# Filler products of TensorE in a planned attention and gated-MLP kernel: one for every 180 planned idle nanoseconds in place of one for every 300

## The chip, the cores and the metric

The kernel runs on one core of one Trainium2 chip. The metric is the device time of one execution in microseconds (us); less is better. The engines of a core are named here as the profile names them: PE is the matmul unit (PEld its weight loads), DVE the vector engine, ACT the scalar engine, POOL is GpSimd, and SP only issues transfers (DMAs) between the main memory and the core's SBUF. Each engine takes its instructions strictly in the order of the program and waits for others through semaphores.

## What is computed

The reference is an attention with a local window and block summaries, and behind it a two-layer MLP in which half of the hidden units are mixed along the sequence and multiplied into the other half. The shapes are batch 4, 8 heads, sequence 768, head size 64; model width 512, hidden width 1024.

```python
# attention, per batch and head
k_sum = k.reshape(B, H, nb, 32, D).max(axis=3)
v_sum = v.reshape(B, H, nb, 32, D).mean(axis=3)
scores_l = where(|i - j| < 16, scale * q @ k.T, -1e9)
scores_s = scale * q @ k_sum.T + log(32)
a = softmax(concat([scores_l, scores_s]))
x = a @ concat([v, v_sum])                 # heads side by side: (4, 768, 512)
# MLP
h = relu(x @ w_in); u, v = h[..., :512], h[..., 512:]
v_n = (v - mean(v)) / sqrt(var(v) + 1e-6)
v_s = w_spatial @ v_n + b_spatial[:, None]
out = (u * v_s) @ w_out
```

## The kernel before

The kernel does not issue its instructions as it goes. It records every operation (a block of matmuls, one vector instruction, one DMA) in a plan, with an estimated duration for each engine that can do it, and then writes the operations out in an order that a long string of characters (`ORDER`) fixes, engine and all. For each operation the plan also keeps a start and an end by its own estimates; they do not change the order, since the order is listed.

For each batch, the attention goes in groups: a group is 256 rows of the sequence and four heads. A group has a block of scores on PE (named s, line 497: 16 small products of q and k), a softmax on DVE (line 510, reading the scores), ACT (line 514, the exponential) and POOL, DVE or ACT (line 527 or 525, the division), a transposition on PE (t, lines 546 and 554), and the product with the values on PE (x, line 570). Then come the MLP's products in float32 split into a high and a low part, three matmuls for one (line 604): pv and pu are the two halves of `x @ w_in`, sp the product with `w_spatial`, po the one with `w_out`.

At the start of the program, before the first MLP product can run, PE has only a few small things to do, and they need transfers and preparations:

- s_0_0, the scores of the first group, needs two blocks of keys (k), into which ACT copies block maxima (line 414), and a block of queries (qd).
- s_1_0 are the scores of a second group. Its queries go to the same buffer as those of s_0_0, so SP issues their load only when s_0_0 is done.
- wwi_3, wwi_1, wwi_0 and wwi_2 are short products (lines 314 to 316) that help to split pieces of `w_in`.
- s_0_1 needs another block of queries (in the second buffer, qd_127 below) and two more blocks of keys.
- vsum (line 441) are sums of the values over blocks, in two halves of 12 products each, read from tiles vn; ACT spreads the result into the tile ve (line 457), which x_0_0 needs. From x_0_0 come xh and xl (lines 273 and 585), which the first pv needs.

SP's loads wait in one row: a load behind one that waits does not start either.

Where the plan sees PE idle between two operations, it puts filler products into PE's row: an identity matrix times its own first 120 columns, into a PSUM tile named warm that nobody reads. The first such product is an operation of its own (line 798) and so is the last (line 869, recorded in the loop over groups, which bounds the stretch of the program in which fillers are put); those between them are written in this loop, at line 910:

```python
    for op in plan.order():
        if op.eng == "PE":
            if warm.made is not None and op.start < warm.ops[-1].start:
                for _ in range(int((op.start - idle - (WARM_0 if idle < WARM_0 else 0)) * WARM)):
                    nc.tensor.matmul(out=warm.t[:, :KW], lhsT=ident, rhs=ident[:, :KW], start=True, stop=True)
            idle = op.end
        op.fn(op.eng)
```

Here `op.start` and `idle` are the plan's estimates in ns, `WARM` is the number of fillers for one ns of planned idle time, and `WARM_0` is taken off the first wait. The profile counts two records for each filler product, since a float32 matmul is done in two passes there.

Of the kernel before, what the change touches and what calls it, by code (L numbers as in the profile page):

```python
# [925 lines left out]
PACE_0, PACE, DENSE_0, STRETCH = 12.13, 15.16, 59.674, 1.249  # L926
WIN_V, WIN_U, WSP_AT, WO_AT = -10.0, 46.367, 71.69, 99.123
VT_OFF, VM_OFF, KP_OFF = 7.652, 3.17, -8.814
WARM, WARM_0, WARM_TO = 1 / 300, 3400.0, 1
ON_PE = (0, 1, 2, 3)  # L930
PAIRED_FROM, HALVED_FROM, AFTER = 6, 2, 8.0
KEEP_AT, MIX_AT = 90.0, 2.0
# [150 lines left out]
```

## Time and profile before

| | |
|---|---|
| time, median of 3 runs | 392.02 us (391.38 to 392.37) |
| the profiled execution's own time | 392.32 us |
| its span, first to last instruction | 390.6 us |
| mean granted TensorE clock over the span | 0.996 |
| busy share: PE, DVE, ACT, POOL | 97%, 74%, 56%, 36% |
| records of filler products (lines 798, 910, 869) | 2, 78, 2 |

The span is what the profile's clock sees between the first and the last instruction; the time of an execution has 1.7 us more around it. Times in the trace count from the span's start. A busy time of PE counts overlapping records once, and the duration of one matmul record includes its passage through the array, so two that follow each other start closer together than either lasts. Where a stretch of the first 6.7 us is asked for, the granted clock reads 1.00 because the record of the clock begins later; the pace of the products tells it there.

### The profile page before, as it was taken

Reading aid. Unit: us, or ns where it says so; the run is one execution under the profiler, and the core shown is the slowest. Engines: PE = TensorE matmul, PEld = TensorE weight load, DVE = VectorE, ACT = ScalarE, POOL = GpSimd, SP = SyncE. Lnnn points to the kernel's source line nnn. Section 1 sums busy time; section 2 is a strip of 40 time slices with the busy share of each in tenths; the row PEclk is TensorE's granted clock in tenths of the full one; section 3 lists DMA queues with packets and bytes.
Section 4 is the critical chain, followed back from the end, with each engine's and each line's share of the span. In section 5 each row is a group of like instructions: output and inputs, shape, how many; then the busy total and the mean of one; then the engine's idle time right before and its main releaser. Section 6 shows DMA issues by size and latency. Waiting matters only on the chain.

```text
span 390.6 us, 9728 instructions
## 1 busy us (share of the span) xinstructions
PE 380.1 (97%) x3547; PEld 331.0 (85%) x3547; DVE 289.6 (74%) x990; ACT 218.2 (56%) x699; POOL 139.6 (36%) x157
## 2 busy tenths in 40 slices
PE   8978999999999999999999999999999999999996
PEld 7656778899989888899897888899998878899985
DVE  3987999999847799975777677886597656754830
ACT  3977998996764594567444493272357454210011
POOL 4222566612532447254051033357345142221210
PEclk9989999999999999999999999999999999999999
DMA  8997868857477898889954795558871343049413
GB/s 312 297 271 213 255 216 273 241 173 221 132 233 259 284 284 295 292 254 309 309 190 165 222 256 180 143 145 253 292 200 27 121 153 109 0 159 306 141 68 122
DMA packets 41983, 81.77 MB, mean 209 GB/s; under 512 B 4560, under 2 KB 17360, under 8 KB 41936
## 3 DMA queue, kind: packets, MB, share of 16 engines
q1 hardware_dynamic: 41792, 81.02, 65.8%
q8 instruction: 28, 0.46, 0.5%
q14 instruction: 19, 0.16, 0.1%
q10 hardware_dynamic: 144, 0.13, 0.1%
HBM read 66.58 MB, written 14.55 MB: 208 GB/s over the span
## 4 chain that ended last, share of the span: by engine, by line
PE 91%; DMA 4%; DVE 2%; ACT 1%; issue 1%; SPq 1%; POOL 0%; ACTq 0%; DVEq 0%; POOLq 0%
PE sp L604 22%; PE pv L604 17%; PE pu L604 17%; PE po L604 16%; PE x L570 6%; PE s L497 5%; PE t L554 3%; DMA qd<-in_qT_dram 2%; PE warm L910 2%; DMA tr<-mixed_w 2%; PE vsum L441 1%; SPq L267 1%; ACT ve L457 0%; DVE vs L652 0%; DVE p L510 0%
## 5 line engine op out<-in xcount | busy, mean ns | idle before, releaser
L514 ACT ACTIVATE p<-p,sums 128x120 f32<-128x120 f32 x192 | 73.9, 387 | 29.4 <-DVE sums L510 29.0
L510 DVE CUSTOM_DVE_ANT_0 p<-s,mask 128x120 f32<-128x120 f32 x192 | 45.9, 275 | 17.7 <-PE s L497 17.5
L604 PE MATMUL pu<-xh,win_h 128*128 128x256 f32 (+1 forms) x128 | 43.5, 340 | 0.4 <-DVE c L746 0.4
L604 PE MATMUL pu<-xl,win_h 128*128 128x256 f32 (+1 forms) x128 | 43.0, 336 | 0.0
L604 PE MATMUL pu<-xh,win_l 128*128 128x256 f32 (+1 forms) x128 | 43.0, 336 | 0.0
L604 PE MATMUL po<-wo_h,gh 128*128 128x512 f32 (+1 forms) x100 | 38.7, 387 | 0.2 <-DVE ob L273 0.2
L604 PE MATMUL pv<-win_h,xh 128*128 128x512 f32 x96 | 38.7, 403 | 0.0
L604 PE MATMUL po<-wo_l,gh 128*128 128x512 f32 (+1 forms) x100 | 38.2, 382 | 0.0
L604 PE MATMUL po<-wo_h,gl 128*128 128x512 f32 (+1 forms) x100 | 38.2, 382 | 0.0
L604 PE MATMUL pv<-win_h,xl 128*128 128x512 f32 x96 | 37.6, 392 | 0.3 <-DVE xl L585 0.3
L604 PE MATMUL sp<-tr,vnh 128*128 128x384 f32 x144 | 37.3, 339 | 0.4 <-DMA tr<-mixed_w 0.4
L604 PE MATMUL pv<-win_l,xh 128*128 128x512 f32 x96 | 37.5, 391 | 0.0
L514 ACT ACTIVATION_READ_ACCUMULATOR p<-p,sums 128x1 f32 x192 | 36.4, 189 | 0.0
L604 PE MATMUL sp<-tr,vs 128*128 128x384 f32 x162 | 30.8, 337 | 0.0
L527 POOL TENSOR_TENSOR p<-p,sums 128x480 f32<-128x480 f32 x20 | 19.7, 991 | 29.2 <-DVE wi L299 9.3
L639 POOL TENSOR_TENSOR mv<-mv,mhalf 128x1 f32<-128x1 f32 x24 | 13.5, 566 | 44.4 <-DVE mv L638 43.6
L277 ACT ACTIVATE u<-pu 128x384 f32<-128x384 f32 (+2 forms) x36 | 13.3, 385 | 28.4 <-PE pu L604 27.2
L570 PEld LDWEIGHTS x<-pt,ve 120*64 120x64 f32 x768 | 23.8, 138 | 5.9 <-issue 5.3
L604 PEld LDWEIGHTS sp<-tr,vs 128*128 128x128 f32 x162 | 27.7, 188 | 0.6 <-DMA tr<-plain 0.4
L604 PEld LDWEIGHTS pu<-xh,win_h 128*128 128x128 f32 x128 | 24.1, 189 | 3.8 <-DVE c L746 0.7
L570 PE MATMUL x<-pt,ve 120*64 120x64 f32 x768 | 25.8, 224 | 1.1 <-issue 1.1
L604 PEld LDWEIGHTS sp<-tr,vnh 128*128 128x128 f32 x144 | 25.5, 188 | 1.4 <-DMA tr<-mixed_w 0.7
(174 smaller groups left out, 935.1 us busy)
## 6 DMA issues: line engine op xcount, KB each, us to landing
tr<-mixed_w SPq DMA_DIRECT2D x36, 384.0 KB, 4.3
tr<-plain SPq DMA_DIRECT2D x27, 384.0 KB, 4.3
k<-in_kext_dram SPq DMA_DIRECT2D x16, 544.0 KB, 5.2
qd<-in_qT_dram SPq DMA_DIRECT2D x24, 256.0 KB, 3.5
ve<-in_vext_dram SPq DMA_DIRECT2D x23, 256.0 KB, 5.2
out_dram<-ob SPq DMA_DIRECT2D x23, 256.0 KB, 2.3
vt<-in_vT_dram SPq DMA_DIRECT2D x48, 96.0 KB, 3.0
wi<-in_w_in_dram SPq DMA_DIRECT2D x7, 512.0 KB, 6.3
```

The costliest lines, as they stand in the source:

```text
L267: add(("SP", issue), lambda e: nc.sync.dma_start(out=out_() if callable(out_) else out_, in_=in_() if callable(in_) else in_), pri, w, r, ...
L277: nc.scalar.activation(out=out_, in_=in_, func=AF.Relu)
L441: nc.tensor.matmul(out=ps.t[pr * SBLK:pr * SBLK + NS, :P], lhsT=vs_one[:, o:o + NS], rhs=vn[t].t[:, pr * P:(pr + 1) * P], start=t == 0, st ...
L497: nc.tensor.matmul(out=ps.t[r * QB:(r + 1) * QB, a, i * KW:(i + 1) * KW], lhsT=qt[hs, r, i], rhs=kts[r].t[hs, g * SEG:g * SEG + KW], start ...
L510: add(("DVE", 203), lambda e, i=i, mi=mi: nc.vector.tensor_tensor_reduce(out=pt.t[:, i, :], in0=ps.t[:, a, i * KW:(i + 1) * KW], in1=mask[ ...
L514: add(("ACT", 380), lambda e, i=i: nc.scalar.activation(out=pt.t[:, i, :], in_=pt.t[:, i, :], func=AF.Exp, scale=-1.0, bias=st.t[:, 0, i:i ...
L527: eng(e).tensor_tensor(out=pt.t, in0=pt.t, in1=st.t[:, 0, :BPU].unsqueeze(2).broadcast_to([P, BPU, KW]), op=ALU.mult)
L554: nc.tensor.transpose(out=ps.t[:KW, r, a * CH + i * QB:a * CH + (i + 1) * QB], in_=pts[a].t[hs, i, :], identity=ident[hs, hs])
L570: nc.tensor.matmul(out=ps.t[a * D:(a + 1) * D, r, n * QB:(n + 1) * QB], lhsT=win(buf, n, o), rhs=rhs(n, a, r), start=True, stop=True)
L604: nc.tensor.matmul(out=ps.t[:, :n], lhsT=x, rhs=y, start=(j == i == 0), stop=(j == last and i == 2))
L639: add(("POOL", 560), lambda e: nc.gpsimd.tensor_tensor(out=mv.t[:, 1:2], in0=mv.t[:, 1:2], in1=mhalf, op=ALU.pow), pri, w=[mv])
L910: nc.tensor.matmul(out=warm.t[:, :KW], lhsT=ident, rhs=ident[:, :KW], start=True, stop=True)
```

## The change

One number in a table of constants is changed: the plan puts a filler product into PE's row for every 180 ns of planned idle time, and not for every 300 ns.

```diff
 PACE_0, PACE, DENSE_0, STRETCH = 12.13, 15.16, 59.674, 1.249
 WIN_V, WIN_U, WSP_AT, WO_AT = -10.0, 46.367, 71.69, 99.123
 VT_OFF, VM_OFF, KP_OFF = 7.652, 3.17, -8.814
-WARM, WARM_0, WARM_TO = 1 / 300, 3400.0, 1
+WARM, WARM_0, WARM_TO = 1 / 180, 3400.0, 1
 ON_PE = (0, 1, 2, 3)
```

Apart from the fillers, each engine has the same instructions in the same order; only the numbers in buffer names differ. Line 910 gives 39 products before and 66 with the change, in these places of PE's row: 19 and 31 before s_0_0, 5 and 9 behind it, 7 and 12 behind s_1_0, 4 and 6 behind the first half of t_0_0, 4 and 7 behind the first half of vsum, and 0 and 1 before the first product of pv_0.

The start of PE's row, before the change (s_0_0 is the block of scores of the first group, wwi_3 a helper product for the weights):

```order
L798 MATMUL warm<-ident 128x120
L910 MATMUL warm<-ident 128x120 x19
L497 MATMUL s_0_0_181<-k_0_136,qd_126 64x120
...
L910 MATMUL warm<-ident 128x120 x5
L314 MATMUL wwi_3_0_222<-wi_2_138,ident 128x512
```

And with the change:

```order
L798 MATMUL warm<-ident 128x120
L910 MATMUL warm<-ident 128x120 x31
L497 MATMUL s_0_0_193<-k_0_136,qd_126 64x120
...
L910 MATMUL warm<-ident 128x120 x9
L314 MATMUL wwi_3_0_238<-wi_2_138,ident 128x512
```

Nothing changed its place; 12 products more stand between the start and s_0_0, and 4 more behind it.

Further down PE's row, from t_0_0 (the transposition of the first group's softmax) to wwi_2, before the change (s_0_1 is the third block of scores, vsum the sums of values from tiles vn):

```order
L546 MATMUL t_0_0_330<-ident,p_0_0_1_205 120x128 x4
L910 MATMUL warm<-ident 128x120 x4
L497 MATMUL s_0_1_349<-k_2_144,qd_127 64x120
...
L546 MATMUL t_0_0_330<-ident,p_0_0_0_200 120x128 x4
L441 MATMUL vsum<-vn_236,vs_one 24x128 x2
L441 MATMUL vsum<-vn_212,vs_one 24x128 x2
L441 MATMUL vsum<-vn_273,vs_one 24x128 x2
...
L910 MATMUL warm<-ident 128x120 x4
L314 MATMUL wwi_2_0_421<-wi_2_138,ident 128x512
```

And with the change:

```order
L546 MATMUL t_0_0_351<-ident,p_0_0_1_217 120x128 x4
L910 MATMUL warm<-ident 128x120 x6
L497 MATMUL s_0_1_372<-k_2_144,qd_127 64x120
...
L546 MATMUL t_0_0_351<-ident,p_0_0_0_212 120x128 x4
L441 MATMUL vsum<-vn_252,vs_one 24x128 x2
L441 MATMUL vsum<-vn_224,vs_one 24x128 x2
L441 MATMUL vsum<-vn_289,vs_one 24x128 x2
...
L910 MATMUL warm<-ident 128x120 x7
L314 MATMUL wwi_2_0_447<-wi_2_138,ident 128x512
```

Two products more stand before s_0_1, three more before wwi_2; vn_273 of before is vn_289 now.

SP's row of loads near the start, which the change leaves as it is but for buffer numbers (in brackets what a load waits for: PE is the end of s_0_0, whose queries the load of qd_126 overwrites; the DMAHW entries are earlier loads):

```order
L267 DMA k_2_144<-in_kext_dram 128x1088
L267 DMA qd_126<-in_qT_dram 128x512 [waits DMAHW3_49,PE_49]
L267 DMA vt_0_0_207<-in_vT_dram 128x192 [waits DMAHW0_49]
L267 DMA vn_212<-in_vnat_dram 128x512 [waits DMAHW1_49]
L267 DMA wi_2_138<-in_w_in_dram 128x1024 [waits DMAHW2_49]
L267 DMA k_3_228<-in_kext_dram 128x1088
L267 DMA vn_232<-in_vnat_dram 128x256 [waits DMAHW4_49]
L267 DMA vn_236<-in_vnat_dram 128x512 [waits DMAHW5_49]
L267 DMA qd_127<-in_qT_dram 128x512 [waits DMAHW6_49]
```

Nothing moved in this row. The load of qd_127, which s_0_1 reads, is the seventh behind the load that waits for s_0_0.

## Rows read from the trace of the kernel before

**Rows 1.** The page, part 1: busy time, share of the span, instructions.

```profile
PE 380.1 (97%) x3547; PEld 331.0 (85%) x3547; DVE 289.6 (74%) x990; ACT 218.2 (56%) x699; POOL 139.6 (36%) x157
```

**Rows 2.** Waits of PE from 40 us on: total, times, longest, us.

```profile
PE pu L604 <- DVE c L746: 0.4, 1, 0.4
PE sp L604 <- DMA tr<-mixed_w: 0.4, 1, 0.4
PE x L570 <- issue: 0.4, 1, 0.4
PE po L604 <- DVE ob L273: 0.2, 1, 0.2
```

**Rows 3.** Timeline of PE, 0 to 36.8 us: start, length, instruction, [idle before].

```profile
2.29 6.54 PE L910 MATMUL warm<-ident 128*128 128x120 f32 x38
8.76 1.05 PE L497 MATMUL s<-k,qd 64*64 64x120 f32 x32
9.74 1.38 PE L910 MATMUL warm<-ident 128*128 128x120 f32 x10
10.95 1.03 PE L314 MATMUL wwi<-wi,ident 128*128 128x512 f32 x2
...
12.88 1.05 PE L497 MATMUL s<-k,qd 64*64 64x120 f32 x32 [0.43 <-DMA qd<-in_qT_dram]
13.86 1.82 PE L910 MATMUL warm<-ident 128*128 128x120 f32 x14
15.52 1.03 PE L314 MATMUL wwi<-wi,ident 128*128 128x512 f32 x2
...
18.49 0.65 PE L546 MATMUL t<-ident,p 128*120 128x128 f32 x4 [0.16 <-POOL p L527]
18.98 1.05 PE L910 MATMUL warm<-ident 128*128 128x120 f32 x8
22.48 1.17 PE L497 MATMUL s<-k,qd 64*64 64x120 f32 x32 [2.45 <-DMA qd<-in_qT_dram]
...
24.43 2.76 PE L441 MATMUL vsum<-vn,vs_one 128*24 128x128 f32 x24
27.12 1.19 PE L910 MATMUL warm<-ident 128*128 128x120 f32 x8
28.15 1.03 PE L314 MATMUL wwi<-wi,ident 128*128 128x512 f32 x2
...
29.56 1.50 PE L441 MATMUL vsum<-vn,vs_one 128*24 128x128 f32 x24
31.79 1.25 PE L570 MATMUL x<-pt,ve 120*64 120x64 f32 x32 [0.73 <-issue]
...
36.05 0.50 PE L604 MATMUL pv<-win_h,xl 128*128 128x512 f32 x1 [0.35 <-DVE xl L585]
```

**Rows 4.** Timeline of ACT: the later of two copies of maxima into k.

```profile
8.15 0.42 ACT L414 COPY k<-gm 128x288 f32<-128x288 f32 x1
```

**Rows 5.** Windows, line 910 alone: stretch, its length, busy (records), granted clock.

```profile
2.60:6.40 3.80, 3.80 (x20) 3.80 (x20) 1.00 0.96 372
7.00:8.40 1.40, 1.40 (x15) 1.40 (x14) 1.00 1.03 416
```

**Rows 6.** Windows, PE alone: stretch, its length, busy (records), granted clock, DMA share.

```profile
23.85:27.20 3.35, 3.35 (x29) 0.50 1.00 256
27.25:31.00 3.75, 3.75 (x36) 1.00 0.85 242
```

**Rows 7.** Timeline of SP: the load of qd behind s_0_0's end.

```profile
9.87 0.33 SPq L267 DMA_DIRECT2D qd<-in_qT_dram  x1
```

**Rows 8.** The chain that ended last, 0 to 60 us: start, length, what.

```profile
13.09 9.25 DMA qd<-in_qT_dram
```

**Rows 9.** Tile vn, loads issued from 21 to 21.5 us, and their time to landing.

```profile
L267 SPq DMA_DIRECT2D vn<-in_vnat_dram x1: 328/328/328, 21.1 to 21.1; - x1
...
DMA to landing us min/median/max: 3.7/3.7/3.7
```

## Prediction

> **What bounds the kernel now.** I read four things in this order: how busy PE is, what it waits for once the MLP runs, its timeline over the first 37 us, and the clock it was granted there. PE is busy for 380.1 us of the span of 390.6 [rows 1]. From 40 us on it waits four times for anything that the profile names, 1.4 us in all (0.4 + 0.4 + 0.4 + 0.2) [rows 2]. So behind 40 us there is almost nothing into which a delay could sink: if the first pv starts d later, the end is about d later too. The fillers all lie before that, and their price is what they do to the start of x_0_0 and, through it, of pv.
>
> Over the first 37 us the reader should look for the idle time in brackets: 0.43 us before s_1_0, 0.16 before t_0_0, 2.45 before s_0_1, 0.73 before x_0_0 and 0.35 inside the first pv [rows 3]. There is none before s_0_0: the fillers run from 2.29 us up to it, and it starts at 8.76. The last of its operands in the rows is ACT's copy into k, which ends at 8.15 + 0.42 = 8.57 us [rows 4]. So the 19 fillers of before fill the wait for s_0_0 to within 0.2 us.
>
> **What one filler costs.** Of the rows at the full clock, the group of 14 records takes 15.52 - 13.86 = 1.66 us until the next instruction and the group of 10 takes 10.95 - 9.74 = 1.21 [rows 3]: 0.45 us for 4 records, 0.1125 each, 0.225 us a product. At the start the pace is slower: 3.8 us hold 20 records there, against 15 in 1.4 us later [rows 5], which is the ratio of the two clock levels, 1.2 and 2.4 GHz. The added 12 come last in their group, behind the time at which the pace has doubled, so I cost them at 0.225. At the slow pace (some 0.42 a product, from the same 3.8 us) they would cost 5.0 us and not 2.7; that is the upper bound of this term.
>
> **The change, place by place**, each shift against the rows of before:
>
> 1. 12 fillers before s_0_0: 12 x 0.225 = 2.70 us, with no idle time to hide them. s_0_0 starts at 11.46.
> 2. The load of the second qd_126 waits for s_0_0's end and holds up all of SP's row behind it. Its issue moves from 9.87 [rows 7] to 12.57.
> 3. 4 fillers more behind s_0_0, 0.90: wwi_3 is 3.60 late, s_1_0 can go at 12.45 + 3.60 = 16.05. Its queries took 12.88 - 9.87 = 3.0 us from issue to use [rows 3, 7] and are there by 15.6. The wait of 0.43 is gone; s_1_0 is 3.17 late.
> 4. 5 fillers more, 1.13: wwi_1 and wwi_0 are 4.30 late. t_0_0's operand comes from a softmax that follows s_0_0, about 18.49 + 2.70 = 21.2, ahead of PE at 18.33 + 4.30 = 22.63; the 0.16 is gone too, and t_0_0 is 4.14 late.
> 5. 2 fillers more, 0.45: PE is ready for s_0_1 at 22.48 - 2.45 + 4.14 + 0.45 = 24.62, where it was ready at 20.03.
> 6. s_0_1 waits for qd_127, issued at 13.09 and landed 9.25 us later, at 22.34 [rows 8]. This issue stands behind that of point 2, so it moves by up to 2.70. The loads between start on emptier queues now, which gives something back; no row shows how much. At one end nothing is given back, 2.70. At the other the load goes as freely as that of point 3 (3.0 us): then it lands before PE wants it, and PE's 24.62 sets s_0_1. I take 2.5, near the first end, since 9.25 us between issue and landing say that the loads ahead of it fill the time, and they all move alike. It lands at 24.84 and s_0_1 starts at about 24.98, 2.50 late, with an idle time of 0.4 in place of 2.45.
> 7. What is given back: the idle time before s_0_1 is followed by a stretch at a granted clock of 0.50, 23.85 to 27.20, and 1.00 after it [rows 6]; these are 1.2 and 2.4 GHz. From s_0_1's start to the end of the first half of vsum is 27.12 - 22.48 = 4.64 us there. At the full clock the same takes 0.98 (s, as 9.74 - 8.76) + 0.49 (t, 18.98 - 18.49) + 1.50 (the second half of vsum) = 2.97 [rows 3]. Keeping the clock is worth 1.67 us, and with the idle time at 0.4 I expect it kept.
> 8. But vsum's third tile is the vn load issued at 21.1 and landed 3.7 later, at 24.8 [rows 9]. Moved by 2.5, it lands at 27.3; PE wants it at 24.98 + 0.98 + 0.49 + 0.50 = 26.95 and waits 0.35. The first half of vsum ends at 28.30, 1.18 late.
> 9. 3 fillers more, 0.68: wwi_2 and the second half of vsum are 1.86 late, and with them ACT's spreading, x_0_0 and pv.
> 10. The one before pv_0, 0.225 us, lies inside the wait of 0.35 for xl [rows 3]. Without that cover it would cost its 0.225.
>
> The sum is 2.70 + 0.90 - 0.43 + 1.13 - 0.16 + 0.45 = 4.59 on PE up to s_0_1, less 2.09 of the idle time there (2.45 - 0.36), less 1.67 of clock, plus 0.35 of a new wait, plus 0.68: **1.86 us**. The profiled execution took 392.32 us, 0.30 over the median of the runs; by its own time the changed kernel gives 394.2, and against the median 393.9. With the loads at their free end, PE sets s_0_1 at 24.62, the wait in point 8 goes, and the sum is (24.62 - 22.48) - 1.67 + 0.68 = 1.15. With the loads 2.70 late it is 2.06.
>
> **A rule against this forecast.** PE's long idle time comes before a stretch at half the clock [rows 3, 6]. The Trainium skill (TensorE: Matmul & The Clock Gate, "Why this matters for your kernels") advises to keep TensorE busy between bursts, because it falls to the low clock when it idles. By that advice alone, denser fillers win the 1.67 us; the trace agrees about the clock and disagrees about the fillers being free, since s_0_0 has no idle time before it. The result it would give is the last rival.
>
> **The rivals.**
>
> - *The clock falls all the same.* The waits of 0.4 and 0.35 us might come together with more, if vn lands later than I take it. Then point 7 is lost: 1.86 + 1.67 = 3.5 us, 395.5. For it: the rows don't tell how short an idle time is short enough. Against: the idle time shrinks from 2.45 to under 1. Chance 0.14. The upper bound of the first term lies in its direction too: with the clock rising later than in this execution, up to 2.3 us more (5.0 - 2.7).
> - *No measurable change.* The loads behind s_0_0 catch up and the clock is kept, 1.15 us; and if the clock rises a microsecond or two earlier than in this execution, the longer first group gains about half of that, where before s_0_0 could not start ahead of its operands: 392.0 to 393.1. For it: emptier queues. Against: the 9.25 us of qd_127's load. Chance 0.23.
> - *Faster.* The fillers lie in waits, as the plan meant, and the clock is kept. It needs s_0_0's operands to come 2.7 us later than in this trace, so that the first 12 cost nothing: 1.15 - 2.70 = -1.55, 390.5. From operands 2.4 us later on the sum is past -1.2, faster. Against it: the copy at 8.15 follows loads that nothing in the change touches. Chance 0.05.
>
> **How the numbers follow.** The forecast as worked out (1.15 to 2.06, that is 393.2 to 394.1) has 0.58. A measurement of this kernel can tell about 0.3%, 1.2 us, from no change. The forecast lies above that mark, with its lower end on it: I count 0.52 of its 0.58 as slower and 0.06 as the same. Slower is then 0.52 + 0.14 = 0.66, the same 0.06 + 0.23 = 0.29, faster 0.05. The range leaves out the faster case and the upper end of the first rival: 392.4 to 395.8.
>
> **What would show it.** In the profile of the changed kernel: s_0_0 at about 11.5 us, directly behind the fillers; the second qd load issued near 12.6; s_0_1 near 25.0 with under 1 us of idle time before it; a granted clock of 1.00 from 22 to 30 us; vsum's first half under 2.2 us long; x_0_0 near 33.6 in place of 31.79; and from there the same waits as before. The prediction is wrong if s_0_0 starts before 10.5 us (its operands, not the fillers, held it), if qd_127 lands within 1.5 us of 22.34 (the loads caught up), if the 0.50 stretch is there again, or if x_0_0 is late by what I say and the end is not, which would mean that PE's waits behind 40 us hide more than the rows name.

## The result, and the profile after

The changed kernel takes 394.50 us (median of 9 runs, 393.73 to 395.67) against 390.25 for the kernel before (9 runs, 388.99 to 392.37, the three known beforehand among them): a ratio of 1.0097, 95% interval 1.0077 to 1.0118. Run again later beside other kernels (e9 below) it took 393.44 against 391.04, a ratio of 1.0065 (1.0041 to 1.0089). So it is slower, by 0.4 to 1.2% with both intervals taken together. The forecast was 393.9, a loss of 1.86 us. The measured time lies in its range, but the loss by medians is 4.25 us the first time and 2.40 the second. That 394.50 comes near 393.9 is luck: the three runs known beforehand lay in the upper part of what the kernel before does, so the forecast started 1.77 us too high (392.02 in place of 390.25), and its loss was 2.39 too small.

The profiled execution of the changed kernel took 394.12 us, 1.80 more than that of before. The page has PE busier by 4.9 us [rows 1] and a granted clock of 0.9 or more in every slice; over the span its mean is 1.00:

```profile
PE 385.0 (98%) x3601; PEld 336.1 (86%) x3601; DVE 289.2 (74%) x990; ACT 217.7 (55%) x699; POOL 139.7 (36%) x157
...
PEclk9999999999999999999999999999999999999999
```

The timeline of PE, beside [rows 3]:

```profile
2.28 9.09 PE L910 MATMUL warm<-ident 128*128 128x120 f32 x62
11.30 1.05 PE L497 MATMUL s<-k,qd 64*64 64x120 f32 x32
12.28 2.27 PE L910 MATMUL warm<-ident 128*128 128x120 f32 x18
14.39 1.03 PE L314 MATMUL wwi<-wi,ident 128*128 128x512 f32 x2
...
15.81 1.05 PE L497 MATMUL s<-k,qd 64*64 64x120 f32 x32
16.79 2.94 PE L910 MATMUL warm<-ident 128*128 128x120 f32 x24
...
22.22 0.60 PE L546 MATMUL t<-ident,p 128*120 128x128 f32 x4
22.66 1.50 PE L910 MATMUL warm<-ident 128*128 128x120 f32 x12
24.09 1.05 PE L497 MATMUL s<-k,qd 64*64 64x120 f32 x32
...
25.65 1.50 PE L441 MATMUL vsum<-vn,vs_one 128*24 128x128 f32 x24
27.07 1.82 PE L910 MATMUL warm<-ident 128*128 128x120 f32 x14
28.73 1.03 PE L314 MATMUL wwi<-wi,ident 128*128 128x512 f32 x2
...
32.38 1.25 PE L570 MATMUL x<-pt,ve 120*64 120x64 f32 x32 [0.73 <-issue]
...
36.66 0.51 PE L604 MATMUL pv<-win_h,xl 128*128 128x512 f32 x1
```

The brackets between s_0_0 and x_0_0 are gone: PE computes fillers where it had waited for 0.43, 0.16 and 2.45 us. s_0_0 is 2.54 us late, s_0_1 1.61, x_0_0 only 0.59. Between s_0_1 and the first half of vsum's end the clock gives back what the forecast said (2.98 us, 24.09 to 27.07, in place of 4.64); the stretch that was at 0.50 [rows 6] is at 1.00:

```profile
23.85:27.20 3.35, 3.35 (x64) 1.00 0.97 274
```

SP issues the load behind s_0_0 2.54 us late [rows 7], and the load of qd_127, issued at 16.4, lands 6.4 us later, at 22.8, where it took 9.25 before [rows 8]; timeline of SP, and the tile qd in the window 16 to 17 us:

```profile
12.41 0.33 SPq L267 DMA_DIRECT2D qd<-in_qT_dram  x1
```

```profile
L267 SPq DMA_DIRECT2D qd<-in_qT_dram x1: 430/430/430, 16.4 to 16.4; - x1
...
DMA to landing us min/median/max: 6.4/6.4/6.4
```

Of the 1.80 us at the end, 0.59 are there at x_0_0, and the other 1.2 come later, 0.9 of them between 66 and 96 us of the trace of before. In that stretch ACT waits 2.13 us for a block of w_spatial, and a pu product waits for ACT, which did not stand among PE's waits before [rows 2]; but all the waits of PE that the profile names add up to 1.4 us in both kernels. The timeline of ACT near 71 us, and the waits of PE from 40 us on:

```profile
70.92 0.84 ACT L273 CAST wsp_h<-ws 128x768 fp32r<-128x768 f32 x1 [2.13 <-DMA ws<-in_w_sp_dram]
```

```profile
PE pu L604 <- ACT vf L277: 0.4, 1, 0.4
PE pu L604 <- DVE c L746: 0.4, 1, 0.4
PE sp L604 <- DMA tr<-mixed_w: 0.4, 2, 0.2
PE po L604 <- DVE ob L273: 0.2, 1, 0.2
```

### The profile page after: what moved, and what is told of

Same layout as the page of the kernel before. It is cut to its first block, busy times and chain, and to the rows that moved or that the text cites. A ratio compares the mean times of both kernels' runs of the same rounds, so it can differ in the third digit from the quotient of the medians.

```text
span 392.4 us, 9836 instructions
## 1 busy us (share of the span) xinstructions
PE 385.0 (98%) x3601; PEld 336.1 (86%) x3601; DVE 289.2 (74%) x990; ACT 217.7 (55%) x699; POOL 139.7 (36%) x157
## 4 chain that ended last, share of the span: by engine, by line
PE 82%; DVE 7%; ACT 5%; DMA 4%; issue 1%; POOL 0%; SPq 0%; ACTq 0%; DVEq 0%; POOLq 0%
PE sp L604 22%; PE po L604 15%; PE pu L604 14%; PE pv L604 13%; PE x L570 5%; PE s L497 4%; PE warm L910 4%; PE t L554 2%; DMA tr<-mixed_w 2%; DMA ws<-in_w_sp_dram 1%; ACT p L514 1%; DVE p L510 1%; PE wwi L314 1%; DVE gm L401 1%; DMA vt<-in_vT_dram 1%
```

## The experiments

All but the first replace the rule for the number of fillers by a list, one number for each of the six places in the order of PE's row (before s_0_0; behind it; behind s_1_0; before s_0_1; before wwi_2; before pv_0). The kernel before is (19, 5, 7, 4, 4, 0), the change (31, 9, 12, 6, 7, 1). Line 910's product is at line 911 there.

```diff
-WARM, WARM_0, WARM_TO = 1 / 300, 3400.0, 1
+WARM, WARM_0, WARM_TO = 1 / 180, 3400.0, 1
+FILL = (31, 5, 7, 4, 4, 0)
...
-    idle = 0
+    idle, fill = 0, list(FILL)
...
-                for _ in range(int((op.start - idle - (WARM_0 if idle < WARM_0 else 0)) * WARM)):
+                n = int((op.start - idle - (WARM_0 if idle < WARM_0 else 0)) * WARM)
+                for _ in range(fill.pop(0) if n > 0 else 0):
```

This table has every kernel: starts in us in the one profiled execution of each, its span, and the time over all runs with the ratio to the kernel before that ran beside it. The ratio is an estimate over all runs and not the quotient of the two medians, which is 1.0033 for e7, where the ratio is 1.0015. The medians of before are 390.47 us for e1 to e4, 390.14 for e5 to e8, 391.04 for e9 to e11: the same kernel differs by 0.9 us between them, so a difference of medians of less than that says little. e6 has four runs, the others from e2 on 10 or 12.

| kernel | fillers | s_0_0 | s_0_1 | x_0_0 | span | median us | ratio (95%) |
|---|---|---|---|---|---|---|---|
| before | 19, 5, 7, 4, 4, 0 | 8.76 | 22.48 | 31.79 | 390.6 | 390.25 | 1 |
| change | 31, 9, 12, 6, 7, 1 | 11.30 | 24.09 | 32.38 | 392.4 | 394.50 | 1.0097 (1.0077 to 1.0118) |
| e1 before again | 19, 5, 7, 4, 4, 0 | 8.54 | 21.68 | 29.66 | 389.1 | 390.79 | one run |
| e2 first only | 31, 5, 7, 4, 4, 0 | 11.87 | 23.85 | 31.68 | 389.8 | 392.21 | 1.0032 (1.0005 to 1.0059) |
| e3 rest only | 19, 9, 12, 6, 7, 1 | 9.23 | 22.01 | 30.31 | 389.7 | 391.26 | 1.0007 (0.9982 to 1.0033) |
| e4 idle only | 19, 5, 7, 13, 4, 0 | 9.12 | 22.33 | 29.97 | 389.5 | 391.45 | 1.0021 (0.9998 to 1.0045) |
| e5 none | 0, 0, 0, 0, 0, 0 | 8.79 | 21.61 | 30.04 | 389.2 | 390.35 | 0.9992 (0.9957 to 1.0027) |
| e6 first 55 | 55, 5, 7, 4, 4, 0 | 15.89 | 27.86 | 35.61 | 394.6 | 397.65 | 1.0168 (1.0117 to 1.0219) |
| e7 twelve behind | 19, 17, 7, 4, 4, 0 | 9.21 | 22.56 | 30.31 | 388.4 | 391.41 | 1.0015 (0.9989 to 1.0042) |
| e8 hidden only | 19, 9, 12, 6, 4, 0 | 8.93 | 21.72 | 29.36 | 388.0 | 391.64 | 1.0032 (1.0002 to 1.0061) |
| e9 change again | 31, 9, 12, 6, 7, 1 | 10.50 | 23.29 | 31.59 | 391.9 | 393.44 | 1.0065 (1.0041 to 1.0089) |
| e10 first and hidden | 31, 9, 12, 6, 4, 0 | 11.19 | 23.99 | 31.63 | 391.6 | 393.30 | 1.0060 (1.0030 to 1.0089) |
| e11 first and last | 31, 5, 7, 4, 7, 1 | 10.82 | 22.83 | 31.24 | 390.8 | 392.83 | 1.0055 (1.0031 to 1.0079) |

**e1: the kernel before, unchanged.**

> The kernel of before, unchanged, for a second profile. Theory 1 (the clock splits its executions): the runs of before lie at 389.0 to 390.3 us and at 391.4 to 392.4; the profiled one took 392.3 and has 3.4 us at a granted clock of 0.50 behind the idle time before s_0_1. If this look takes about 389.3, its clock shows no such stretch, and vsum's first half takes 1.5 us and not 2.8; if it takes about 392, the stretch is there again. Rival (the split is not the clock): a look at 389.3 with the stretch in it, or one at 392 without.

It took 390.79 us, between the two groups that I had seen in nine runs. The timeline of PE and a window of it (the number behind the records is the granted clock):

```profile
21.68 1.17 PE L497 MATMUL s<-k,qd 64*64 64x120 f32 x32 [1.85 <-DVE win_h L273]
23.36 1.73 PE L441 MATMUL vsum<-vn,vs_one 128*24 128x128 f32 x24
...
29.66 1.25 PE L570 MATMUL x<-pt,ve 120*64 120x64 f32 x32 [0.73 <-issue]
```

```profile
21.70:25.00 3.30, 3.25 (x60) 1.00 0.90 280
```

PE again sits idle before s_0_1, for 1.85 us, and the clock stays at 1.00. The row names a copy on DVE, which s_0_1 does not read; the load of qd_127, issued at 13.05, lands 8.5 us later, at 21.6. x_0_0 comes 2.13 us earlier than in the profile of before. The theory that the clock splits the executions of before falls: 82 runs of before beside the experiments have a mean granted clock from 0.995 to 1.000 each, only two of them under 0.998, where the profiled execution with the half-speed stretch has 0.996 (those two took 392.58 and 392.76 us); and their times are spread over 388.9 to 393.8 us without two groups. The stretch on which the forecast built is rare.

**e2 and e3: the first place alone, and all the others alone.** FILL = (31, 5, 7, 4, 4, 0) and (19, 9, 12, 6, 7, 1).

> 31 fillers before s_0_0 as in the change, the other places as before (5, 7, 4, 4, 0). Theory 1 (the first 12 carry the loss, because nothing hides them and SP's row waits for s_0_0): s_0_0 near 11.3 us, second load of qd_126 near 12.4, s_0_1 held to 22.8 by its own load as in the change, x_0_0 about 0.5 us later than in an execution of before that keeps its clock; the later loads of w_spatial late as in the change: 391.0 to 393.5 us. Rival (the fillers behind s_0_0 carry it): within 0.5 us of before.

> 19 fillers before s_0_0 as before, the other places as in the change (9, 12, 6, 7, 1). Theory 1: s_0_0 at 8.8; the added 10 products before s_0_1 take 2.2 us of which the idle time of 2.45 hides nearly all, and the clock is kept; the 3 behind vsum's first half cost 0.7: at most 0.7 us over an execution of before that keeps its clock, 389.3 to 390.5 us, without executions at 391.4 and over. Rival (these carry the loss): 392 us and over.

Against e1, x_0_0 is 2.02 us late with the first place alone and 0.65 late with the others alone; the change has 2.72, about the sum. By medians the first place costs 1.7 us and the others 0.8, the latter within the measurement. The median of e2 lies where theory 1 put it (391.0 to 393.5), that of e3 above its place (389.3 to 390.5) and below the rival's (392); and x_0_0 of e2 was to be about 0.5 late, not 2.02.

The sum at x_0_0 is partly chance, because s_0_0 does not start at the same time behind the same 19 fillers. In e3 they end before its operands are there, and it waits for ACT; the timeline of PE in e3:

```profile
9.23 1.05 PE L497 MATMUL s<-k,qd 64*64 64x120 f32 x32 [0.65 <-ACT k L414]
```

That is 0.69 us behind e1. Counted from s_0_0, x_0_0 comes 21.12 us later in e1 and 21.08 in e3, so the 0.65 is not shown to be a price of e3's fillers. What speaks for the first place is the row of all kernels: the ratios of those with 19 fillers there (e3, e4, e7, e8) lie from 1.0007 to 1.0032, with 31 (e2, e9, e10, e11, change) from 1.0032 to 1.0097, and with 55 (e6) at 1.0168. e3 and e9 below differ in the first place alone, and their intervals do not touch (up to 1.0033, from 1.0041). So the first 12 carry most of it, as theory 1 says; by their intervals alone e2 is not told apart from any of e3, e4, e7 and e8. The timeline of PE in e2 shows what sets s_0_1 now:

```profile
11.87 1.05 PE L497 MATMUL s<-k,qd 64*64 64x120 f32 x32
...
21.61 0.65 PE L546 MATMUL t<-ident,p 128*120 128x128 f32 x4 [0.49 <-POOL p L527]
...
23.85 1.18 PE L497 MATMUL s<-k,qd 64*64 64x120 f32 x32 [0.70 <-ACT k L414]
```

PE waits again, but for POOL's division and for ACT's copy of the maxima into k, not for a load. DVE and ACT work in the order of the program too, and the softmax of s_0_0 stands ahead of these steps in their rows. From the start of s_0_0 to that of s_0_1 it takes 11.98 us in e2, 11.97 in e6 and 12.01 in e11; where the load of qd_127 comes last it takes 13.72 (before).

**e4: fillers in the long wait alone.** FILL = (19, 5, 7, 13, 4, 0).

> As before, but 13 fillers and not 4 right before s_0_1, where PE sat idle for 2.45 us: 9 more, 2.0 us by their pace, all inside that wait. Theory 1: s_0_1 stays near 22.5 us, no stretch at 0.50 behind it, 389.0 to 389.6 us in every execution. Rival (the clock's fall is not what splits the executions of before): two groups again, as in before, or no change of the median.

No gain: 391.45 us, 1.0021 (0.9998 to 1.0045). It is the expected rival, "no change of the median"; the wait before s_0_1 is filled, as expected, and that is worth nothing where the clock does not fall.

**e5: no fillers.** FILL = (0, 0, 0, 0, 0, 0).

> No filler at all at line 910 (the first one of line 798 and the last of line 869 stay). Theory 1 (what the fillers buy is the clock of the first 30 us, nothing else): s_0_0 starts when its operands are there, 8.6 to 9.2 us, so nothing is won at the start; the short products up to vsum run for some time at a granted clock of 0.50, and x_0_0 comes 1 to 4 us later than the 29.7 us of the second profile of before: 391.5 to 394.5 us. Rival (the fillers of before are themselves partly on the path): x_0_0 earlier, under 390 us.

A miss for theory 1: 390.35 us, as the kernel before; the rival, x_0_0 earlier, did not come either. By the median the fillers of before buy no time that can be measured here, and cost none. The timeline of PE, and two windows:

```profile
8.79 1.88 PE L497 MATMUL s<-k,qd 64*64 64x120 f32 x32 [6.29 <-ACT k L414]
...
13.46 1.82 PE L497 MATMUL s<-k,qd 64*64 64x120 f32 x32
...
21.61 1.86 PE L497 MATMUL s<-k,qd 64*64 64x120 f32 x32 [1.59 <-ACT k L414]
...
30.04 1.25 PE L570 MATMUL x<-pt,ve 120*64 120x64 f32 x32 [0.73 <-issue]
```

```profile
22.00:25.30 3.30, 3.30 (x44) 0.50 1.00 282
25.40:31.00 5.60, 4.87 (x74) 1.00 0.68 198
```

PE idles for 6.29 us before s_0_0. Its first blocks go at about half the pace (s_0_0 takes 1.88 us and s_1_0 1.82, where e1 has 1.05), and it is at half the clock again from 22.0 to 25.3; but the blocks there are short, s_0_0 waits for its operands until 8.79 in any case, and x_0_0 is 0.38 us behind e1. The fillers do hold the clock: without them six of ten runs had a mean clock of 0.996 or less, with them two of 82. Those six took 390.33 to 394.27 us, the four at 1.000 took 388.66 to 390.19, which suggests that the clock is worth something; why the median of e5 is no higher all the same is not shown.

**e6: 55 in the first place.** FILL = (55, 5, 7, 4, 4, 0).

> 55 fillers before s_0_0, 36 more than before and 24 more than in the first-only run, the other places as before. Theory 1 (each filler there costs its 0.222 us once the room is used up): s_0_0 near 16.9 us, x_0_0 some 5.3 us later than the 31.7 of the first-only run, 397.5 us (396.5 to 398.5). Rival (a fixed loss, by SP's row starting late once or by where transfers collide): under 395 us.

397.65 us as expected. The 24 products more than in e2 put s_0_0 4.02 us later and not 5.3, and x_0_0 3.93 later: they cost what they move, and no room is left behind them. The pace doubled earlier in this execution than in e2 (26 records of fillers from 2.6 to 6.4 us against 20), which is the missing 1.3 us. By medians the step from e2 is 5.4 us; the profiled execution is the fastest of the four, 396.30 us.

**e7 and e8: twelve behind s_0_0, and the three hidden places alone.** FILL = (19, 17, 7, 4, 4, 0) and (19, 9, 12, 6, 4, 0).

> The same number of fillers as in the first-only run, but the 12 added ones stand behind s_0_0 (19, then 17). s_0_0 goes at its old time, and with it the load behind it, the softmax and what stands behind the softmax on DVE and ACT. Theory 1 as mended by the first-only run (the loss is the late start of everything that follows s_0_0, not PE's time): the 2.67 us of fillers sink into PE's wait before s_0_1; s_0_1 0.5 to 1.0 us later than in before, and x_0_0 by as much: 390.8 to 391.6 us, below the first-only run. Rival (PE's own time is the loss, wherever the fillers stand): x_0_0 near 31.7 us and 392.2 us, as in the first-only run.

> The change's fillers in the three places between s_0_0 and s_0_1 alone (19, 9, 12, 6, then 4 and 0 as before): 11 products, 2.45 us, all inside PE's wait before s_0_1. Theory 1: x_0_0 within 0.4 us of an execution of before at the same s_0_0, 0.67 us earlier than with the 3 behind vsum's first half; median within 0.3% of before (389.5 to 391.3 us). Rival: as far over before as the run with all places but the first, 0.8 us or more.

In e7 the same twelve products cost 0.65 us at x_0_0 in place of 2.02, and 391.41 us in place of 392.21 by medians. Even the 0.65 is not theirs: s_0_0 came 0.67 us later than in e1, and from s_0_0 to x_0_0 it is 21.10 us against 21.12. PE's time for them sinks into its wait; by the profiles the loss of e2 is that everything behind s_0_0 starts late. The times alone do not show it, since the intervals of e2 and e7 overlap. In e8 the profile bears out theory 1, with the earliest x_0_0 of all. Its median does not: 391.64 us, 1.0032 (1.0002 to 1.0061), is above what theory 1 allowed (391.3), 1.5 us over before and so on the rival's side, with the same ratio as e2. This is not settled. PE's timelines of e7 and of e8:

```profile
9.21 1.05 PE L497 MATMUL s<-k,qd 64*64 64x120 f32 x32
...
22.56 1.17 PE L497 MATMUL s<-k,qd 64*64 64x120 f32 x32 [0.27 <-ACT k L414]
...
30.31 1.25 PE L570 MATMUL x<-pt,ve 120*64 120x64 f32 x32 [0.73 <-issue]
```

```profile
8.93 1.05 PE L497 MATMUL s<-k,qd 64*64 64x120 f32 x32 [0.26 <-ACT k L414]
...
21.72 1.05 PE L497 MATMUL s<-k,qd 64*64 64x120 f32 x32
...
29.36 1.25 PE L570 MATMUL x<-pt,ve 120*64 120x64 f32 x32 [0.73 <-ACT ve L457]
```

**e9, e10 and e11: the change again, and the first place with each half of the others.** FILL = (31, 9, 12, 6, 7, 1), (31, 9, 12, 6, 4, 0) and (31, 5, 7, 4, 7, 1).

> The change once more (31, 9, 12, 6, 7, 1), beside the next two on one chip. In the profiles so far, the start of x_0_0 adds up: against the second profile of before 2.02 us for the first place alone, 0.65 for all the others, 2.72 for the change. In the medians it does not: 1.7 and 0.8 us, but 4.0 for the change. Theory 1 (PE's delay at x_0_0 is all there is, the rest is spread between executions): about 393.2 us this time. Rival (the places together cost more than apart): 394.0 us or more again.

> 31 fillers before s_0_0, and the change's numbers in the three places up to s_0_1 (9, 12, 6), then 4 and 0 as before. The room before s_0_1 is needed twice: the first 12 have used most of it, so the 11 products there should not be hidden any more. If room is what counts: s_0_1 near 24.1 to 24.6 us directly behind the fillers, x_0_0 at 31.9 to 32.4, 393 to 394 us. If not: as the first-only run, 31.7 and 392.2.

> 31 fillers before s_0_0, then 5, 7, 4 as before, then 7 and 1 as in the change. Theory 1: x_0_0 at 31.7 + 0.67 = 32.4 us, 0.7 us over the first-only run: 392.9 us (392.2 to 393.6). Rival (loss by the pairing of places): as high as the change, 394 us and over, or no more than the first-only run.

e9 came near what theory 1 gave, 393.44 for 393.2; the excess of the first measurement did not come back in full. e10 shows that the room before s_0_1 is needed twice: s_0_1 follows the fillers directly, 12.80 us behind s_0_0 (12.79 in the change and in e9) where e2 needs 11.98, so the 11 products cost about 0.8 us there once the first 12 have made the loads come early enough. Its x_0_0 at 31.63 is below what was expected for that case and no later than in e2, because s_0_0 started 0.68 earlier. e11 lies at 392.83 as expected, but its x_0_0 came at 31.24 and not at 32.4, with s_0_0 1.05 us earlier than in e2. Counted from s_0_0 the prices are plain: x_0_0 follows 19.81 us later in e2, 20.44 in e10 (0.63 more for the 11 products), 20.42 in e11 (0.61 more for the three behind vsum), 21.08 in the change and 21.09 in e9 (1.27 and 1.28 more for both).

## Why the prediction was right, and where it was not

The direction and the mechanism of the first five points of the sum hold, each a little smaller than forecast. Twelve fillers before s_0_0 have almost nothing to hide in: 2.54 us of 2.70 in this pair of executions. Over all profiles it is less: s_0_0 starts at 8.97 us on the mean of the six with 19 fillers and at 11.14 on that of the five with 31, 2.17 later. In three of the six (e3, e4, e8) s_0_0 had waited for ACT's copy for 0.65, 1.22 and 0.26 us behind the fillers, and the sum had put this room at nothing from one execution. The load behind s_0_0 was issued at 12.41 (12.57 forecast), s_1_0 started at 15.81 (16.05) without its wait, and t_0_0 at 22.22 (22.63) without its own. Point 9 holds: from the end of vsum's first half to wwi_2 there are 1.66 us (28.73 - 27.07) where e1 has 0.99 (26.01 - 25.02), 0.67 more for three products. Point 10 holds: the wait of 0.35 for xl is gone, with the one product in it.

Points 6 and 8 failed. The load of qd_127 was to land 2.5 us late and landed 0.5 late: issued 3.3 us later, it took 6.4 us in place of 9.25. That is no exception: in e9, e10, e11 and e2, issued from 15.3 to 16.7 us, it took 5.4 to 5.9, and in e1, issued at 13.1, 8.5. The forecast had named this as a sign of error ("the loads caught up"). So PE itself set s_0_1, at 24.09, vsum did not wait, and by the profiles the sum at x_0_0 was 0.59, below even the lower bound of 1.15. Part of that bound was off because PE was ready for s_0_1 earlier than I put it. I had taken the end of the last filler's record as the moment at which PE is ready, and that end includes the product's passage through the array: in the change s_0_1 starts at 24.09, while the record of the fillers ahead of it lasts until 24.16 (22.66 + 1.50). The same happened at s_1_0, which starts 0.07 us before the end of the record ahead of it, and at t_0_0, with 0.16; with the 0.16 that were missing at s_0_0 already this is most of the way from 24.62 to 24.09.

The step that failed in substance is point 7. The 1.67 us of returned clock are real in this pair of profiles, but the kernel before rarely loses them: e1 has an idle time of 1.85 us there and no stretch at 0.50, and at most two of 82 runs had a mean clock as low as the profiled one. Against e1 the change is 2.72 us late at x_0_0 and e9 1.93, and the loss that the second measurement shows is between them (2.40 us). A price of 1.86 that nets a common loss against a rare gain is too small for the median.

That the profiled executions differ by 1.80 us, as the sum said, is therefore chance: 0.59 of it is in place at x_0_0 and 1.2 come later. The time from x_0_0 to the end of the span runs from 358.1 (e2, e7) to 360.3 us (e9) over the thirteen profiles; the change, e9 and e10 are the three highest, at 360.0, 360.3 and 360.0. The long wait for a block of w_spatial does not tell them apart: the waits of ACT from 60 to 80 us, in e4 first and then in e9 (total, times, longest):

```profile
ACT wsp_h L273 <- DMA ws<-in_w_sp_dram: 2.1, 1, 2.1
ACT wsp_h L273 <- DMA ws<-in_w_sp_dram: 0.3, 1, 0.3
```

e4 waits as long as the change (2.1 us) without being among the three, and e9 hardly waits. Two executions of the kernel before drift against each other nearly as much. The first x block behind 90 us starts at these times in before, in e1 and in the change (timelines of PE, 90 to 100 us):

```profile
96.26 2.08 PE L570 MATMUL x<-pt,ve 120*64 120x64 f32 x64
94.85 2.08 PE L570 MATMUL x<-pt,ve 120*64 120x64 f32 x64
97.78 2.09 PE L570 MATMUL x<-pt,ve 120*64 120x64 f32 x64
```

So e1, which was 2.13 us ahead of before at x_0_0, is 1.41 ahead there, a shift of 0.7 with the same fillers, and the change, 0.59 behind, is 1.52 behind, a shift of 0.9. Whether the three highest share a cause or fall there by chance stays open, and with it the difference between 4.25 and 2.40 us in the two measurements of the change.

## What to carry to other kernels

A filler on an engine that works strictly in order is free only up to the moment at which the next real operation has its operands; here 19 products filled that wait to within 0.2 us in one execution and left up to 1.22 us of it in another, and everything that waits for the operation, a row of loads and the other engines' rows, moved with it. Before a change is credited with a faster clock, look at whether the slow stretch is there in other executions: the mean clock of each run tells. And measure what the existing fillers are worth by leaving them out; here they held the clock, and the median showed no difference (0.9992, 0.9957 to 1.0027). A place counted from the start of the span carries the luck of everything ahead of it; counted from the last common event, here s_0_0, the prices of the fillers added up to within 0.04 us.

## What the runs showed of the hardware

The pace of the first products doubles at a different time in each execution, and the start of s_0_0 behind the same 31 fillers moves with it: 10.50, 10.82, 11.19, 11.30 and 11.87 us in e9, e11, e10, the change and e2. The records of fillers from 2.6 to 6.4 us and from 7.0 to 8.4 show it, first e9, then e2:

```profile
2.60:6.40 3.80, 3.80 (x27) 3.80 (x27) 1.00 0.99 396
7.00:8.40 1.40, 1.40 (x15) 1.40 (x14) 1.00 1.04 423
```

```profile
2.60:6.40 3.80, 3.80 (x20) 3.80 (x20) 1.00 0.98 380
7.00:8.40 1.40, 1.40 (x11) 1.40 (x11) 1.00 1.04 424
```

The long wait of PE before s_0_1 came before a stretch at 0.50 in one execution of before (2.45 us idle) and before none in the other (1.85 us idle); in e5, where PE had no fillers, 1.59 us idle at that place came before one too. And one and the same program, on one core, spreads over 388.9 to 393.8 us, 1.3%, in the 82 runs of before.
